# Banded attention on pairs of heads, woven slot by slot into the two products of an MoE layer

## The chip, the cores and the metric

One core of one Trainium2 chip runs the whole program. The metric is the device time of one execution in microseconds (us), the median of three runs. The core has five engines with a queue each: TensorE (PE; its weight loads are listed as PEld), VectorE (DVE), ScalarE (ACT), GpSimd (POOL) and SyncE (SP), which here only issues DMAs. Each takes its instructions in order and waits on semaphores for the others.

## The reference

Attention over 8 batches, 8 heads, 576 positions of 64 values, where a position sees itself and the 63 before it; then, on the concatenated heads, `(h - tanh(h)) @ w_out` with `h = x @ w_in`:

```python
scores = scale * np.matmul(q, k.transpose(0, 1, 3, 2))
mask = (rel >= 0) & (rel < 64)            # rel = query position - key position
scores = np.where(mask, scores, -1000000000.0)
scores = scores - np.max(scores, axis=-1, keepdims=True)
attn = np.exp(scores)
attn = attn / (np.sum(attn, axis=-1, keepdims=True) + 1e-09)
out = np.matmul(attn, v)                  # x: 4608 tokens of 512 values
h = x @ w_in                              # 512 x 2048
g = h - np.tanh(h)
result = g @ w_out                        # 2048 x 512, in float32
```

## The kernel before, in words

Two stages follow each other. Tile's scheduler and its pools set the order of instructions on each engine within a stage.

**Attention** (L66 to L128) goes through 64 heads. Per head GpSimd issues 15 DMAs that load and cast k, v and q in blocks of 128 rows (L78 to L80; each is one entry on the POOL queue). TensorE transposes k and q block by block (`tp`, L84 and L87), VectorE copies the transposes to `kT` and `qT` (L85, L88). Then five query tiles: scores `sc` (L101, 64 values deep), the band mask added on VectorE (L103), exp with row sums on ScalarE (L106), reciprocal and scaling on VectorE (L109, L110), one or two transposes of the probabilities (`tpp`, L119) with copies (`pt_sb`, L121), one or two products with v (`ov`, L126), and a copy into `xT` on ScalarE (L128). `xT` holds all 4608 tokens, transposed.

**MoE** (L138 to L154) goes through 9 chunks of 512 tokens. For each of 16 blocks of d_ff four 512-column products make `hp` (L142), ScalarE takes the tanh (`th`, L145), VectorE the difference (`gT`, L146). For each of four token blocks 16 products make `yp` (L150), ScalarE copies it to `ysb` (L153), and SyncE issues the store (L154). `hp` and `yp` have two PSUM banks each. Both weights are loaded first of all, by one DMA each on the POOL queue (L51, L53).

Of the kernel before, what the change touches and what calls it, by code (L numbers as in the profile page):

```python
# [1 line left out]

# [13 lines left out]
@with_exitstack
def kernel(
    ctx: ExitStack,
    tc: tile.TileContext,
    q: bass.AP,  # L20
    k: bass.AP,
    v: bass.AP,
    moe_w_in: bass.AP,
    moe_w_out: bass.AP,
    out: bass.AP,
):
# [20 lines left out]
    nc.gpsimd.affine_select(bmask, bmask, compare_op=ALU.is_gt, fill=-1e9,
                            base=0, pattern=[[1, 192]], channel_multiplier=-1)

    w_in_sb = const.tile([128, 4, d_ff], BF16)  # L50
    nc.gpsimd.dma_start(out=w_in_sb, in_=moe_w_in.rearrange("(ko ki) f -> ki ko f", ki=128))  # L51
    w_out_sb = const.tile([128, 16, d_model], BF16)
    nc.gpsimd.dma_start(out=w_out_sb, in_=moe_w_out.rearrange("(ko ki) f -> ki ko f", ki=128))  # L53

    xT = const.tile([128, 4, NT], BF16)

    scale = 1.0 / (D ** 0.5)

    attn_stack = ExitStack()
    kv_pool = attn_stack.enter_context(tc.tile_pool(name="kv", bufs=2))  # L60
    qt_pool = attn_stack.enter_context(tc.tile_pool(name="qt", bufs=2))
    ps_pool = attn_stack.enter_context(tc.tile_pool(name="ps", bufs=1, space=bass.MemoryType.PSUM))
    ps2_pool = attn_stack.enter_context(tc.tile_pool(name="ps2", bufs=2, space=bass.MemoryType.PSUM))
    sm_pool = attn_stack.enter_context(tc.tile_pool(name="sm", bufs=3))

    for b in range(B):  # L66
        for h in range(H):
            ksb = kv_pool.tile([128, NB, D], BF16)
            vsb = kv_pool.tile([128, NB, 128], BF16)
            pi0 = (h % 2) * 64  # L70
            po = h // 2
            nc.vector.memset(vsb, 0.0)
            qsb = kv_pool.tile([128, NB, D], BF16)
            kT = qt_pool.tile([64, S], BF16)
            qT = qt_pool.tile([64, S], BF16)
            for ib in range(NB):
                r = 128 if ib < 4 else 64
                nc.gpsimd.dma_start(out=ksb[:r, ib, :], in_=k[b, h, ib*128:ib*128+r, :])  # L78
                nc.gpsimd.dma_start(out=vsb[:r, ib, pi0:pi0+64], in_=v[b, h, ib*128:ib*128+r, :])  # L79
                nc.gpsimd.dma_start(out=qsb[:r, ib, :], in_=q[b, h, ib*128:ib*128+r, :])  # L80
            for ib in range(NB):
                r = 128 if ib < 4 else 64
                tp = ps_pool.tile([64, 128], BF16)
                nc.tensor.transpose(tp[:, :r], ksb[:r, ib, :], ident[:r, :r])  # L84
                nc.vector.tensor_copy(kT[:, ib*128:ib*128+r], tp[:, :r])  # L85
                tp2 = ps_pool.tile([64, 128], BF16)
                nc.tensor.transpose(tp2[:, :r], qsb[:r, ib, :], ident[:r, :r])  # L87
                nc.vector.tensor_copy(qT[:, ib*128:ib*128+r], tp2[:, :r])  # L88

            for t in range(5):  # L90
                if t == 0:
                    q0, sq, k0, sk = 0, 64, 0, 64
                    mask = cmask
                else:
                    q0 = 64 + 128 * (t - 1)
                    sq = 128
                    k0 = 128 * (t - 1)
                    sk = 192
                    mask = bmask
                sc = ps2_pool.tile([128, 192], F32)  # L100
                nc.tensor.matmul(sc[:sq, :sk], qT[:, q0:q0+sq], kT[:, k0:k0+sk],  # L101
                                 start=True, stop=True)
                nc.vector.tensor_tensor(sc[:sq, :sk], sc[:sq, :sk], mask[:sq, :sk], ALU.add)  # L103
                p_sb = sm_pool.tile([128, 192], BF16)
                rs = sm_pool.tile([128, 1], F32)
                nc.scalar.activation(p_sb[:sq, :sk], sc[:sq, :sk], ACT.Exp,  # L106
                                     scale=scale, accum_out=rs[:sq, :])
                rsi = sm_pool.tile([128, 1], F32)
                nc.vector.reciprocal(rsi[:sq, :], rs[:sq, :])  # L109
                nc.vector.tensor_scalar(p_sb[:sq, :sk], p_sb[:sq, :sk], rsi[:sq, :],  # L110
                                        None, ALU.mult)
                ov = ps2_pool.tile([128, 128], F32)
                nks = (sk + 127) // 128
                pts = []
                for j in range(nks):
                    c0 = j * 128
                    cw = min(128, sk - c0)
                    tpp = ps_pool.tile([128, 128], BF16)
                    nc.tensor.transpose(tpp[:cw, :sq], p_sb[:sq, c0:c0+cw], ident[:sq, :sq])  # L119
                    pt_sb = sm_pool.tile([128, 128], BF16)  # L120
                    nc.vector.tensor_copy(pt_sb[:cw, :sq], tpp[:cw, :sq])  # L121
                    pts.append((pt_sb, c0, cw))
                for j, (pt_sb, c0, cw) in enumerate(pts):
                    kb = (k0 + c0) // 128
                    ko = (k0 + c0) % 128
                    nc.tensor.matmul(ov[:, :sq], vsb[ko:ko+cw, kb, :], pt_sb[:cw, :sq],  # L126
                                     start=(j == 0), stop=(j == nks - 1))
                nc.scalar.activation(xT[pi0:pi0+64, po, b*S+q0:b*S+q0+sq], ov[pi0:pi0+64, :sq], ACT.Copy)  # L128

    attn_stack.close()  # L130
    mp = ctx.enter_context(tc.tile_pool(name="mp", bufs=2, space=bass.MemoryType.PSUM))
    mp2 = ctx.enter_context(tc.tile_pool(name="mp2", bufs=2, space=bass.MemoryType.PSUM))
    gpool = ctx.enter_context(tc.tile_pool(name="gp", bufs=2))
    opool = ctx.enter_context(tc.tile_pool(name="op", bufs=3))
    TOK = 512
    for nb in range(NT // TOK):
        t0 = nb * TOK
        gT = gpool.tile([128, 16, TOK], BF16)  # L138
        for m in range(16):
            hp = mp.tile([128, TOK], F32)  # L140
            for ki in range(4):
                nc.tensor.matmul(hp, w_in_sb[:, ki, m*128:(m+1)*128],  # L142
                                 xT[:, ki, t0:t0+TOK], start=(ki == 0), stop=(ki == 3))
            th = opool.tile([128, TOK], F32)
            nc.scalar.activation(th, hp, ACT.Tanh)  # L145
            nc.vector.tensor_tensor(gT[:, m, :], hp, th, ALU.subtract)  # L146
        for s in range(4):
            yp = mp2.tile([128, d_model], F32)
            for m in range(16):
                nc.tensor.matmul(yp, gT[:, m, s*128:(s+1)*128], w_out_sb[:, m, :],  # L150
                                 start=(m == 0), stop=(m == 15))
            ysb = opool.tile([128, d_model], F32)
            nc.scalar.activation(ysb, yp, ACT.Copy)  # L153
            nc.sync.dma_start(out=out[t0+s*128:t0+(s+1)*128, :], in_=ysb)  # L154


# [28 lines left out]
```

## Time and profile before

| | us |
|---|---|
| median of three runs | 896.19 (896.13 to 896.44) |
| span of the profiled execution | 894.0 |
| attention, first to last product | 26.0 to 629.8 |
| MoE, first product to end | 629.8 to 894.0 |
| TensorE busy | 756.3 |
| VectorE busy | 534.9 |
| ScalarE busy | 311.1 |
| GpSimd busy | 513.1 |

The profile is one execution. Its page gives busy time by engine, the span in 40 slices, the chain of work that ended last, the costliest groups of instructions by line, and the DMAs. "Idle before, releaser" in a row names what ended the idle time of the engine just before. Products on TensorE overlap, and their ends are modelled, so the distance of two starts tells more than a duration.

### The profile page before, as it was taken

Reading aid. Unit: us, or ns where it says so; the run is one execution under the profiler, and the core shown is the slowest. Engines: PE = TensorE matmul, PEld = TensorE weight load, DVE = VectorE, ACT = ScalarE, POOL = GpSimd, SP = SyncE. Lnnn points to the kernel's source line nnn. Section 1 sums busy time; section 2 is a strip of 40 time slices with the busy share of each in tenths; the row PEclk is TensorE's granted clock in tenths of the full one; section 3 lists DMA queues with packets and bytes.
Section 4 is the critical chain, followed back from the end, with each engine's and each line's share of the span. In section 5 each row is a group of like instructions: output and inputs, shape, how many; then the busy total and the mean of one; then the engine's idle time right before and its main releaser. Section 6 shows DMA issues by size and latency. Waiting matters only on the chain.

```text
span 894.0 us, 12015 instructions
## 1 busy us (share of the span) xinstructions
PE 756.3 (85%) x3264; PEld 341.5 (38%) x3264; DVE 534.9 (60%) x2384; ACT 311.1 (35%) x1141; POOL 513.1 (57%) x973
## 2 busy tenths in 40 slices
PE   0688888888888888888888888888999999999998
PEld 0333333333333333333333333333344444444443
DVE  0577777777777777777777777777533443334332
ACT  0233333333333333333333333333434443334433
POOL 3888888888888798798888888876000000000000
PEclk9999999999999999999999999999999999999999
DMA  9533334334333343343333433433011001100011
GB/s 164 52 24 25 25 24 25 25 24 25 24 26 24 23 27 25 23 27 24 24 24 25 25 24 25 25 22 21 1 48 48 25 23 48 48 36 23 36 48 48
DMA packets 133796, 28.62 MB, mean 32 GB/s; under 512 B 126560, under 2 KB 128608, under 8 KB 133728
## 3 DMA queue, kind: packets, MB, share of 16 engines
q0 software_dynamic: 128544, 18.41, 28.6%
q1 hardware_dynamic: 5184, 9.44, 2.8%
q8 instruction: 26, 0.43, 0.2%
q14 instruction: 42, 0.34, 0.1%
HBM read 36.70 MB, written 9.44 MB: 52 GB/s over the span
## 4 chain that ended last, share of the span: by engine, by line
PE 72%; DVE 17%; issue 4%; ACT 3%; DMA 3%; POOL 0%; ACTq 0%; DVEq 0%; POOLq 0%
PE tpp L119 15%; PE yp L150 14%; PE hp L142 14%; PE ov L126 11%; PE sc L101 10%; DVE pt_sb L121 7%; DVE sc L103 5%; PE tp L84 5%; PE tp L87 3%; DMA w_out_sb<-in_moe_w_out_dram 3%; ACT p_sb L106 2%; DVE p_sb L110 2%; DVE rsi L109 1%; DVE gT L146 1%; DVE qT L88 1%
## 5 line engine op out<-in xcount | busy, mean ns | idle before, releaser
L79 POOL DMA_DIRECT2D vsb<-in_v_dram x320 | 193.2, 604 | 85.0 <-DVE kT L85 73.5
L119 PE MATMUL tpp<-ident,p_sb 128*128 128x128 bf16 (+2 forms) x576 | 161.0, 279 | 85.2 <-DVE p_sb L110 40.8
L128 ACT ACTIVATE xT<-ov 64x128 bf16<-64x128 f32 (+1 forms) x320 | 83.3, 260 | 387.0 <-PE ov L126 387.0
L78 POOL DMA_DIRECT2D ksb<-in_k_dram x320 | 200.4, 626 | 17.5 <-issue 8.6
L80 POOL DMA_DIRECT2D qsb<-in_q_dram x320 | 195.5, 611 | 3.8 <-issue 3.8
L146 DVE TENSOR_TENSOR gT<-hp,th 128x512 bf16<-128x512 f32 x144 | 99.5, 691 | 152.6 <-ACT th L145 152.6
L121 DVE COPY pt_sb<-tpp 128x128 bf16<-128x128 bf16 (+2 forms) x576 | 124.6, 216 | 81.5 <-PE tpp L119 52.6
L126 PE MATMUL ov<-pt_sb,vsb 128*128 128x128 bf16 (+2 forms) x576 | 158.2, 275 | 13.8 <-DVE pt_sb L121 0.6
L142 PE MATMUL hp<-xT,w_in_sb 128*128 128x512 bf16 x576 | 147.4, 381 | 4.6 <-DVE gT L146 4.6
L150 PE MATMUL yp<-w_out_sb,gT 128*128 128x512 bf16 x576 | 145.6, 379 | 0.0
L84 PE MATMUL tp<-ident,ksb 128*64 128x128 bf16 (+1 forms) x320 | 96.6, 302 | 26.0 <-DMA ksb<-in_k_dram 26.0
L119 PEld LDWEIGHTS <-p_sb 128*128 128x128 bf16 (+2 forms) x576 | 68.9, 120 | 128.6 <-DVE p_sb L110 61.4
L145 ACT ACTIVATE th<-hp 128x512 f32<-128x512 f32 x144 | 86.0, 597 | 86.1 <-PE hp L142 58.9
L106 ACT ACTIVATE p_sb<-sc 128x192 bf16<-128x192 f32 (+1 forms) x320 | 97.3, 304 | 38.8 <-DVE sc L103 27.6
L126 PEld LDWEIGHTS <-vsb 64*128 64x128 bf16 (+1 forms) x576 | 58.5, 102 | 127.4 <-issue 90.1
L101 PE MATMUL sc<-kT,qT 64*128 64x192 bf16 (+1 forms) x320 | 103.1, 322 | 3.6 <-DVE qT L88 0.5
L103 DVE TENSOR_TENSOR sc<-sc,bmask 128x192 f32<-128x192 f32 x256 | 91.4, 357 | 23.8 <-PE sc L101 23.7
L87 PE MATMUL tp<-ident,qsb 128*64 128x128 bf16 (+1 forms) x320 | 97.2, 304 | 0.7 <-DMA qsb<-in_q_dram 0.6
L85 DVE COPY kT<-tp 64x128 bf16<-64x128 bf16 (+1 forms) x320 | 62.1, 194 | 49.3 <-PE tp L84 49.0
L110 DVE TENSOR_SCALAR p_sb<-p_sb,rsi 128x192 bf16<-128x192 bf16 (+1 forms) x320 | 87.8, 274 | 2.3
L142 PEld LDWEIGHTS <-w_in_sb 128*128 128x128 bf16 x576 | 55.9, 97 | 79.2 <-issue 19.2
L150 PEld LDWEIGHTS <-gT 128*128 128x128 bf16 x576 | 54.8, 98 | 70.3 <-DVE gT L146 6.4
(23 smaller groups left out, 353.8 us busy)
## 6 DMA issues: line engine op xcount, KB each, us to landing
out_dram<-ysb SPq DMA_DIRECT2D x36, 256.0 KB, 2.0
ksb<-in_k_dram POOLq DMA_DIRECT2D x256, 16.0 KB, 2.1
vsb<-in_v_dram POOLq DMA_DIRECT2D x256, 16.0 KB, 2.1
qsb<-in_q_dram POOLq DMA_DIRECT2D x256, 16.0 KB, 2.1
w_in_sb<-in_moe_w_in_dram POOLq DMA_DIRECT2D x1, 2048.0 KB, 13.1
w_out_sb<-in_moe_w_out_dram POOLq DMA_DIRECT2D x1, 2048.0 KB, 22.6
ksb<-in_k_dram POOLq DMA_DIRECT2D x64, 8.0 KB, 2.0
vsb<-in_v_dram POOLq DMA_DIRECT2D x64, 8.0 KB, 2.0
```

Source lines behind the costliest of these rows:

```text
L78: nc.gpsimd.dma_start(out=ksb[:r, ib, :], in_=k[b, h, ib*128:ib*128+r, :])
L79: nc.gpsimd.dma_start(out=vsb[:r, ib, pi0:pi0+64], in_=v[b, h, ib*128:ib*128+r, :])
L80: nc.gpsimd.dma_start(out=qsb[:r, ib, :], in_=q[b, h, ib*128:ib*128+r, :])
L84: nc.tensor.transpose(tp[:, :r], ksb[:r, ib, :], ident[:r, :r])
L87: nc.tensor.transpose(tp2[:, :r], qsb[:r, ib, :], ident[:r, :r])
L101: nc.tensor.matmul(sc[:sq, :sk], qT[:, q0:q0+sq], kT[:, k0:k0+sk], start=True, stop=True)
L103: nc.vector.tensor_tensor(sc[:sq, :sk], sc[:sq, :sk], mask[:sq, :sk], ALU.add)
L119: nc.tensor.transpose(tpp[:cw, :sq], p_sb[:sq, c0:c0+cw], ident[:sq, :sq])
L121: nc.vector.tensor_copy(pt_sb[:cw, :sq], tpp[:cw, :sq])
L126: nc.tensor.matmul(ov[:, :sq], vsb[ko:ko+cw, kb, :], pt_sb[:cw, :sq], start=(j == 0), stop=(j == nks - 1))
L142: nc.tensor.matmul(hp, w_in_sb[:, ki, m*128:(m+1)*128], xT[:, ki, t0:t0+TOK], start=(ki == 0), stop=(ki == 3))
L150: nc.tensor.matmul(yp, gT[:, m, s*128:(s+1)*128], w_out_sb[:, m, :], start=(m == 0), stop=(m == 15))
```

## The change

It replaces the whole body of the kernel. What is computed is the same.

**Attention on head pairs.** Heads `pr` and `pr + 4` of a batch form a pair `g` (32 in all). q and k of a pair come in by two SP DMAs as float32, 96 partitions with six positions each (`load_qk`); GpSimd casts them (`cast_qk`); six transposes each (`tr`) give `qT` by one ScalarE copy and `kTb` by two VectorE copies, in which the keys of the two heads alternate column by column and the other head's half is zero. So one 128x128 product gives the scores of 64 keys of both heads against 128 queries, already transposed (`scores`), exp goes straight into `PT`, and the mask is multiplied in afterwards for all nine blocks at once (`masking`). The products with `vaug` (`pv`) take `PT` as it lies; a column of ones in `vaug` gives the row sums; VectorE multiplies by the reciprocal into `xs`. `x_tr` transposes the result of a batch into chunk tiles `xT`. No maximum is subtracted in either kernel.

**One stream.** `manual_schedule` makes the order of the code the order on each engine. The stream is cut into slots `n`: slot `n` has the four products of one `hp` (chunk `n // 16`), attention steps of the table `early`, four products of `yp` of the chunk before, attention steps of the table `late`. A pair from g = 4 on starts every four slots; four pairs stand ahead of slot 0. I call the four slots of a pair A (`tr`), B (`scores`), C (`masking`, first `pv`) and D (second `pv`). Attention ends with slot 111, `hp` with 143, `yp` with 159. `hp`, scores and transposes have two PSUM banks, `yp` and `ov` one.

```diff
+    ctx.enter_context(tc.manual_schedule())
+    def cast_qk(g):
+        for n in "qk":
+            t = row_pool.tile([P96, E6, 2, D], BF16, tag=n + "b", name=n + "b")
+            nc.gpsimd.tensor_copy(t.rearrange("p e h d -> p h e d"),
+                                  stage.pop((g, n)).rearrange("p h (e d) -> p h e d", d=D))
...
+    def tr(g, which):
...
+        for e in range(E6):
+            nc.tensor.transpose(tp[:, e, :], src[:, e, :], ident[:P96, :P96])
+        if which == "q":
+            nc.scalar.activation(qT[g % NR][:, 0:S].rearrange("c (p e) -> c e p", e=E6), tp, ACT.Copy)
+        else:
+            kt = kTb[g % NR]
+            for i in range(2):
+                nc.vector.tensor_copy(
+                    kt[64 * i:64 * i + 64, :, i].rearrange("c (p e) -> c e p", e=E6),
+                    tp[64 * i:64 * i + 64])
+    def scores(g, grp):
+        sp = ps_s.tile([128, 3, 128], F32, tag="s", name="sp")
+        for i in range(3):
+            j = 3 * grp + i
+            nc.tensor.matmul(sp[:, i, :], kTb[g % NR].rearrange("c t h -> c (t h)")[:, 128 * j:128 * j + 128],
+                             qT[g % NR][:, 64 * j:64 * j + 128], start=True, stop=True)
+        nc.scalar.activation(PT[g % NR][:, 3 * grp:3 * grp + 3, 0:128], sp, ACT.Exp, scale=scale)
+    def masking(g):
+        p = PT[g % NR][:, :, 0:128]
+        nc.vector.tensor_tensor(p, p, mask.unsqueeze(1).to_broadcast([128, NJ, 128]), ALU.mult)
+    def pv(g, t0, t1):
...
+            for i, (j, c0) in enumerate(parts):
+                nc.tensor.matmul(ov[:, t - t0, :], ptf[:, c0:c0 + 128], vaug[b % NV][:, pr, j, :],
+                                 start=(i == 0), stop=(i == len(parts) - 1))
...
+        nc.vector.reciprocal(rc[:, 0:n], ovr[:, :, :, 64:65])
...
+        nc.vector.tensor_tensor(xo, ovr[:, :, :, 0:64], rc[:, 0:n].to_broadcast([128, n, 2, 64]), ALU.mult)
+    def y_out(c, s):
+        ysb = sm_pool.tile([128, d_model], F32, tag="ysb", name="ysb")
+        nc.scalar.activation(ysb, yps[c, s], ACT.Copy)
...
+    LEAD = 18
+    for g in range(NG):
+        b, pr = divmod(g, NP)
+        a = g - 10 if g < NP else 4 * g - LEAD
+        if g >= NP:
+            at(late, a - 10, load_qk, g)
+            at(late, a - 4, cast_qk, g)
+        at(early, a, tr, g, "q")
+        at(late, a, tr, g, "k")
+        at(early, a + 1, scores, g, 0)
+        at(early, a + 1, scores, g, 1)
+        at(late, a + 1, scores, g, 2)
+        at(early, a + 2, masking, g)
+        at(late, a + 2, pv, g, 0, 3)
+        at(late, a + 3, pv, g, 3, 5)
+        if pr == NP - 1:
             for t in range(5):
+                at(early if t % 2 == 0 else late, a + 4 + t // 3, x_tr, b, t)
+            if b + 2 < B:
+                at(late, a + 4, load_v, b + 2)
...
+        if 0 <= c < NC:
+            hp_mm(c, m)
+        for fn in early.get(n, []):
+            fn[0](*fn[1:])
+        if 1 <= c <= NC:
+            yp_mm(c - 1, m)
+        for fn in late.get(n, []):
+            fn[0](*fn[1:])
```

What stood on TensorE before, in the middle of attention (`sc` scores, `tp` and `tpp` transposes, `ov` products with v; in brackets the engine or DMA queue whose semaphore is waited for):

```order
L101 MATMUL sc<-kT,qT 128x192 [waits Activation_49]
L84 LDWEIGHTS ksb [waits DMASW1_49]
L84 MATMUL tp<-ident,ksb 64x64
L119 LDWEIGHTS p_sb
L119 MATMUL tpp<-ident,p_sb 64x128 [waits DVE_49]
L126 LDWEIGHTS vsb
L126 MATMUL ov<-pt_sb,vsb 128x128 [waits PE_49]
```

Nearly every product there has a wait of its own. The same queue now, from the end of slot A to the start of slot C of one pair (`tp` transposes of k, `hp` and `yp` the MoE products, `sp` scores; groups of like products cut to their first):

```order
L151 LDWEIGHTS kb [waits Pool_49]
L151 MATMUL tp<-ident,kb 128x96
...
L212 MATMUL hp<-xT,w_in_sb 128x512 [waits DVE_49]
...
L165 LDWEIGHTS ktb_100 [waits DVE_49]
L165 MATMUL sp<-qt_103,ktb_100 128x128 [waits Activation_49]
...
L226 MATMUL yp<-w_out_sb,gT 128x512
...
L165 MATMUL sp<-qt_103,ktb_100 128x128 [waits Activation_49]
...
L226 MATMUL yp<-w_out_sb,gT 128x512 [waits Activation_49]
```

The waits have moved to the heads of groups, and between the transposes of k and the scores that read them stands one group `hp`. VectorE before, in the same stage (`kT`, `pt_sb` copies, `rsi` reciprocal, `p_sb` scaling):

```order
L109 RECIPROCAL rsi<-rs 128x1 [waits Activation_49]
L103 TENSOR_TENSOR sc<-sc,bmask 128x192 [waits PE_49]
L110 TENSOR_SCALAR p_sb<-p_sb,rsi 128x192 [waits DVE_49]
L85 COPY kT<-tp 64x128 [waits PE_49]
L121 COPY pt_sb<-tpp 128x128 [waits PE_49]
```

and now, one period of four slots (`ktb` the copies of k, `pt` masking, `xs` the scaled result):

```order
L218 TENSOR_TENSOR gT<-hp,th 128x512 [waits Activation_49]
L157 COPY ktb_100<-tp 64x6x96 [waits PE_49]
L157 COPY ktb_100<-tp 64x6x96
L218 TENSOR_TENSOR gT<-hp,th 128x512 [waits Activation_49] x2
L171 TENSOR_TENSOR pt_97<-pt_97,mask 128x9x128
L189 RECIPROCAL rc<-ov 128x6 [waits PE_49]
L191 TENSOR_TENSOR xs_107<-ov,rc 128x6x64 [waits DVE_49]
L218 TENSOR_TENSOR gT<-hp,th 128x512 [waits Activation_49]
L189 RECIPROCAL rc<-ov 128x4 [waits PE_49]
L191 TENSOR_TENSOR xs_107<-ov,rc 128x4x64 [waits DVE_49]
```

VectorE now has eleven operations for a pair of heads and four `hp` groups, where attention alone took 35 for each head. Last, GpSimd at the start. Before:

```order
L51 DMA w_in_sb<-in_moe_w_in_dram 128x4x2048
L47 AFFINE_SELECT bmask<-bmask 128x192 [waits Pool_49]
L53 DMA w_out_sb<-in_moe_w_out_dram 128x16x512
L78 DMA ksb<-in_k_dram 128x64
L79 DMA vsb<-in_v_dram 128x64 [waits DVE_49]
```

and now, from the last of the four first pairs to the cast of the fifth (`vaug` is v, `qb`, `kb` the cast rows):

```order
L77 CAST qb<-qf 96x2x6x64 [waits DMAHW6_49,PE_49]
L77 CAST kb<-kf 96x2x6x64 [waits DMAHW7_49,PE_49]
L132 DMA w_in_sb<-in_moe_w_in_dram 128x4x512 [waits DMASW0_49]
...
L89 DMA vaug_95<-in_v_dram 64x36x64 [waits DMASW4_49,DVE_49]
...
L136 DMA w_out_sb<-in_moe_w_out_dram 128x4x512 [waits DMASW0_49]
L136 DMA w_out_sb<-in_moe_w_out_dram 128x4x512 [waits DMASW1_49]
L77 CAST qb<-qf 96x2x6x64 [waits DMAHW0_49,PE_49,Pool_49]
```

The weights have moved behind the first four pairs, in four pieces each, and the casts of the fifth pair stand behind them.

## Rows read from the trace of the kernel before

**Rows 1.** The page: span, and a DMA group (count, KB each, us to landing).

```profile
span 894.0 us, 12015 instructions
...
ksb<-in_k_dram POOLq DMA_DIRECT2D x256, 16.0 KB, 2.1
```

**Rows 2.** Stretches: length, busy by engine (instructions), granted clock, DMA share, GB/s.

```profile
0.00:26.00 26.00, 0.00 (x0) 0.00 (x0) 0.65 (x2) 1.28 (x1) 7.53 (x20) 1.00 0.99 166
26.00:629.80 603.80, 500.53 (x2112) 230.83 (x2112) 434.66 (x2238) 202.10 (x959) 505.58 (x953) 1.00 0.38 24
632.80:881.00 248.20, 243.59 (x1105) 105.70 (x1104) 98.42 (x143) 104.45 (x175) 0.00 (x0) 1.00 0.09 34
```

**Rows 3.** Timeline of MoE: start, duration, engine, line, instructions, idle before.

```profile
700.78 1.02 PE L142 MATMUL hp<-xT,w_in_sb 128*128 128x512 bf16 x4
701.64 0.38 PE L150 MATMUL yp<-w_out_sb,gT 128*128 128x512 bf16 x1
701.84 0.60 ACT L145 ACTIVATE th<-hp 128x512 f32<-128x512 f32 x1 [0.76 <-DVE gT L146]
...
880.22 9.95 PE L150 MATMUL yp<-w_out_sb,gT 128*128 128x512 bf16 x45
890.26 0.60 ACT L153 ACTIVATE ysb<-yp 128x512 f32<-128x512 f32 x1 [2.90 <-PE yp L150]
```

**Rows 4.** Timeline of TensorE: a pair in attention, the first loads of MoE.

```profile
302.39 0.31 PE L84 MATMUL tp<-ident,ksb 128*64 128x128 bf16 x1
302.49 0.31 PE L87 MATMUL tp<-ident,qsb 128*64 128x128 bf16 x1
...
630.21 0.15 PEld L142 LDWEIGHTS <-w_in_sb 128*128 128x128 bf16 x1 [0.28 <-issue]
630.64 0.15 PEld L142 LDWEIGHTS <-w_in_sb 128*128 128x128 bf16 x1 [0.27 <-issue]
```

**Rows 5.** Instructions by line and shape: count, busy us, mean ns, idle before.

```profile
L146 DVE TENSOR_TENSOR gT<-hp,th 128x512 bf16<-128x512 f32 x144 | 99.5, 691 | 152.6 <-ACT th L145 152.6
L103 DVE TENSOR_TENSOR sc<-sc,bmask 128x192 f32<-128x192 f32 x256 | 91.4, 357 | 23.8 <-PE sc L101 23.7
L145 ACT ACTIVATE th<-hp 128x512 f32<-128x512 f32 x144 | 86.0, 597 | 86.1 <-PE hp L142 58.9 <-DVE gT L146 27.2
L106 ACT ACTIVATE p_sb<-sc 128x192 bf16<-128x192 f32 x256 | 83.4, 326 | 12.5 <-DVE sc L103 2.0
L110 DVE TENSOR_SCALAR p_sb<-p_sb,rsi 128x192 bf16<-128x192 bf16 x256 | 73.1, 286 | 2.3
L121 DVE COPY pt_sb<-tpp 128x128 bf16<-128x128 bf16 x256 | 57.5, 224 | 46.5 <-PE tpp L119 38.4
L109 DVE RECIPROCAL rsi<-rs 128x1 f32<-128x1 f32 x256 | 39.2, 153 | 5.1 <-ACT p_sb L106 1.1
L72 DVE MEMSET vsb<- 128x320 uint32 x64 | 20.8, 325 | 1.8 <-PEq L169 0.9 <-PE tp L84 0.4
L110 DVE TENSOR_SCALAR p_sb<-p_sb,rsi 64x64 bf16<-64x64 bf16 x64 | 14.7, 230 | 0.0
L121 DVE COPY pt_sb<-tpp 64x64 bf16<-64x64 bf16 x64 | 11.7, 182 | 8.6 <-PE tpp L119 0.2
L106 ACT ACT_TABLE_LOAD x1 | 1.3, 1283 | 0.7 <-PEq L169 0.7
L45 POOL TENSOR_SCALAR_AFFINE_SELECT bmask<-bmask 128x192 f32<-128x192 f32 x1 | 0.3, 335 | 0.0
L41 POOL TENSOR_SCALAR_AFFINE_SELECT cmask<-cmask 64x64 f32<-64x64 f32 x1 | 0.2, 228 | 0.0
```

**Rows 6.** Timeline of GpSimd at the start of the program.

```profile
2.89 0.36 POOL L47 TENSOR_SCALAR_AFFINE_SELECT bmask<-bmask 128x192 f32<-128x192 f32 x1
3.18 1.19 POOL L53 DMA_DIRECT2D w_out_sb<-in_moe_w_out_dram  x1
4.90 0.57 POOL L79 DMA_DIRECT2D vsb<-in_v_dram  x1
```

More of the change, by code (lines that the diff above doesn't have):

```diff
@@ L4 @@
 import concourse.tile as tile
-from concourse import bass_utils, mybir
-from concourse.masks import make_identity
+from concourse import mybir
 from concourse._compat import with_exitstack
@@ L47 @@
[L47 to L88, printed above, removed]
-            for t in range(5):
[L91 to L154, printed above, removed]
@@ new lines, with load_qk @@
+    xs = [const.tile([128, 5, d_model], BF16, name=f"xs{i}") for i in range(2)]
+    stage, rows = {}, {}
+    def load_qk(g):
+        b, pr = divmod(g, NP)
+        for n, x in (("q", q), ("k", k)):
+            t = qk_pool.tile([P96, 2, E6 * D], F32, tag=n + "f", name=n + "f")
+            nc.sync.dma_start(out=t, in_=x[b, pr::NP].rearrange("h (p e) d -> p h (e d)", e=E6))
+            stage[g, n] = t
+    def cast_qk(g):
[3 more added lines that the diff above has]
+                                  stage.pop((g, n)).rearrange("p h (e d) -> p h e d", d=D))
+            rows[g, n] = t
@@ new lines @@
+    ones(0)
+    nc.vector.memset(vaug[1], 0.0)
+    ones(1)
+    w_in_r = moe_w_in.rearrange("(ko ki) f -> ki ko f", ki=128)
+    w_out_r = moe_w_out.rearrange("(ko ki) f -> ki ko f", ki=128)
+    for pr in (1, 2, 3):
+        load_v_pair(0, pr)
+        cast_qk(pr)
+    for i in range(4):
+        nc.gpsimd.dma_start(out=w_in_sb[:, :, 512 * i:512 * i + 512],
+                            in_=w_in_r[:, :, 512 * i:512 * i + 512])
+    load_v(1)
+    for i in range(4):
+        nc.gpsimd.dma_start(out=w_out_sb[:, 4 * i:4 * i + 4, :], in_=w_out_r[:, 4 * i:4 * i + 4, :])
@@ new lines, in x_tr @@
+    def x_tr(b, t):
+        tp = ps_tp.tile([128, 4, 128], BF16, tag="tp", name="tpx")
+        for i in range(4):
+            nc.tensor.transpose(tp[:, i, :], xs[b % 2][:, t, 128 * i:128 * i + 128], ident)
+        lo, hi = b * S + 128 * t, b * S + min(128 * t + 128, S)
+        at = lo
+        while at < hi:
+            c = at // TOK
+            to = min(hi, (c + 1) * TOK)
+            nc.vector.tensor_copy(chunk_tile(c)[:, :, at - c * TOK:to - c * TOK],
+                                  tp[:, :, at - lo:to - lo])
+            at = to
@@ new lines, with hp_mm @@
+    gT, yps = {}, {}
+    def hp_mm(c, m):
+        hp = ps_hp.tile([128, TOK], F32, tag="hp", name="hp")
+        for ki in range(4):
+            nc.tensor.matmul(hp, w_in_sb[:, ki, m * 128:(m + 1) * 128], chunk_tile(c)[:, ki, :],
+                             start=(ki == 0), stop=(ki == 3))
+        th = sm_pool.tile([128, TOK], F32, tag="th", name="th")
+        nc.scalar.activation(th, hp, ACT.Tanh)
+        if m == 0:
+            gT[c] = g_pool.tile([128, M, TOK], BF16, tag="gT", name="gT")
+        nc.vector.tensor_tensor(gT[c][:, m, :], hp, th, ALU.subtract)
@@ new lines, in yp_mm @@
+    def yp_mm(c, st):
+        s, part = divmod(st, 4)
+        if part == 0:
+            yps[c, s] = ps_yp.tile([128, d_model], F32, tag="yp", name="yp")
+        for i in range(4):
+            m = 4 * part + i
+            nc.tensor.matmul(yps[c, s], gT[c][:, m, s * 128:(s + 1) * 128], w_out_sb[:, m, :],
+                             start=(m == 0), stop=(m == M - 1))
+    def y_out(c, s):
+        ysb = sm_pool.tile([128, d_model], F32, tag="ysb", name="ysb")
+        nc.scalar.activation(ysb, yps[c, s], ACT.Copy)
+        r0 = c * TOK + s * 128
+        nc.sync.dma_start(out=out[r0:r0 + 128, :], in_=ysb)
@@ L158 @@
+    first = min(min(early), min(late))
+    for n in range(first, 16 * (NC + 1) + 1):
+        c, m = divmod(n, M)
+        if n >= 1:
+            cy, sy = divmod(n - 17, M)
+            if n >= 17 and sy % 4 == 3 and cy < NC:
+                y_out(cy, sy // 4)
+        if 0 <= c < NC:
[6 more added lines that the diff above has]
+            fn[0](*fn[1:])
 _INS = ['q', 'k', 'v', 'moe_w_in', 'moe_w_out']
```

102 lines of the change are left out of this document (89 added, 13 removed).

## The prediction

> **What bounds the kernel now.** I read the page first, then the stretches, then the lines of single instructions. The page gives a span of 894.0 us [rows 1]; the median of the runs is 896.19 us, so 2.2 us lie around the span. The stretches show two programs behind each other [rows 2]: nothing on TensorE until 26.0 us, attention from there to 629.8 us, then the two MoE products to 894. Attention is thus 604 us, and by its 2112 products a step takes 286 ns. It is no bound of throughput: TensorE, VectorE and GpSimd are all 72 to 84% busy there, and each small product is one link in a chain through other engines. MoE is a bound of throughput: 512-column products follow each other at (9.95 - 0.38) / 44 = 0.2175 us, and in the middle of the stage at 0.2155 [rows 3] (45 from 880.22, which end 9.95 us later, the last 0.38 after its start; four from 700.78 to 701.64).
>
> [...]
>
> **The change part by part.** Removed: all 2112 small products and 2238 VectorE operations [rows 2] of attention as a stage of its own. Put in: for each of 32 head pairs 12 transposes of 96 columns, 9 score products of 128 and 13 value products of 130; for each of 8 batches 20 transposes of the result; 1248 products in all. Of the 32 pairs, 28 stand inside the MoE stream, one every four slots, 4 ahead of it. MoE keeps its 1152 products: 1152 x 0.2155 = 248 us, the floor.
>
> Price of a small product. From below 0.2155/4 = 0.054 us (a stream at the upper level), from above 0.105 us (the pair of [rows 4]). I price at the upper level, since every slot of the stream holds eight 512-column products of the kind beside which [rows 3] shows it, and take 0.065, nearer to the lower end, since at neither level do the closest rows show a load that holds up a product. 1248 x 0.065 = 81 us. [...]
>
> Prices on the other engines [rows 5]. ScalarE: 192 columns 0.326, 512 columns 0.597, so 0.85 ns a column: an exp of 384 columns 0.49, the copy of qT (576) 0.65; tanh 0.60, ysb, as many columns, 0.60. One load of a function table served Exp, Tanh and Copy of the whole program [rows 5], so alternating them costs nothing. VectorE: 0.357 at 192 and 0.691 at 512 columns, 1.04 ns a column: gT 0.69, the product with the reciprocal 0.56 and 0.42 with 0.15 for the reciprocal ahead of it. The bf16 copy runs 0.182 at 64 and 0.224 at 128 columns: a copy of 512 columns 0.48; the two kT copies (576 columns, every second element written) between 0.52 and 0.69 each: I take 0.69, because the cheap rows all write neighbouring elements. Masking, 1152 columns: 0.286 at 192 and 0.230 at 64 give 0.71; at 1.04 ns a column it would be 1.29, which the time until its reader covers. GpSimd casts (768 columns) appear in no row: affine-select of 64 and 192 columns at 0.228 and 0.335 gives 0.9; above that I allow 1.8, the double.
>
> One period (four slots, one pair), written out by hand from these prices with 0.2 us from the last product of a group to its reader (tanh at 701.84 follows the fourth of the products from 700.78 at 0.2155 each [rows 3]). Work on TensorE: 32 x 0.2155 + 34 small = 6.9 + 2.0 = 8.9 us. VectorE has 6.7 us, ScalarE 5.1, GpSimd 2 to 4: none is the bound. But TensorE takes its instructions in order, so two waits show. (1) Transposes of k end slot A; two copies of 0.69 and 0.2 latency follow, and only hp of slot B (0.86) stands ahead of the score products that read them: 0.75 us wait. The MoE products of that slot queue behind it. (2) yp has a single bank, its evacuation stands on ScalarE behind the third exp, at the end of slot B; exp ends 0.65 into slot C, ysb 1.25, and yp could start at 0.86: 0.4 us. Masking ends 0.75 ahead of its reader; hp with two banks, ov with one, are free in time. Period 8.9 + 1.15 = about 10.1. Once in four periods five result transposes come in: 1.3 us of products, and their copies stand on VectorE behind gT, with two banks for three users: about 1.4 us more. Sixteen slots: 4 x 10.1 + 2.7 = 43.2 us, 2.7 per slot.
>
> The sum in order. Start to slot 0: before, both weights (4 MB) went first and nothing ran on TensorE until they were in, 26 us at 166 GB/s [rows 2]; now q and k of the first pair (0.59 MB, 3.6 us at that rate, plus the 2.1 that a small DMA takes to land [rows 1]) are in at about 6 us. GpSimd then goes through four pairs, casts and v issues at 0.6 each, 3 us a pair, to 17; ten larger issues, between the 0.57 and the 1.19 of [rows 6], say 0.9 each, and the wait for the second piece of w_in take it to 28, and only then comes the cast of pair 4, whose transposes stand ahead of the first hp: 35 us. VectorE's own chain (memsets of 2.4 by 0.325 for 320 words [rows 5], four pairs of 3.5 with latencies) ends near 29, the lower end; casts at 1.8 give 43. Slots 0 to 15, with no yp as cover: the same chain with 8.5 us a period, 36 (30 to 42). Slots 16 to 111: 96 x 2.7 = 259; TensorE alone at 0.054 gives 212, 0.105 with the same waits 294. Slots 112 to 143: 256 x 0.2155 = 55. Slots 144 to 159: 64 x 0.2155 = 14 and three waits for the single yp bank, 0.86 each: 16. Last evacuation to the end 3.9 (890.26 to the end of the span in [rows 3], and 0.2). Around the span 2. In all 35 + 36 + 259 + 55 + 16 + 4 + 2 = 407 us.
>
> **The rivals.** *Everything hides:* the kT copies cost 0.52, the scheduled distance covers the waits, small products stream at 0.054: 30 + 32 + 220 + 77 = about 360 to 385. For it speaks that no engine but TensorE is near full; against it that the two waits follow from in-order queues and from durations of the trace. *Another wait takes over:* masking has two operands in SBUF and runs while GpSimd casts. In the trace of before, GpSimd only issues DMAs after 3.25 us [rows 6], so no row shows the two together. If a mask had to wait out one or both casts (0.9 to 1.8 each), less the 0.75 of slack, that is up to 1 us, or 2.9, in each of 28 pairs: 435 to 485. [...] Against the rival: a cast is released by transposes of slot A and should be done before the mask at the start of slot C. [...] *Slower than before:* GpSimd's cast, the one operation with no row of its kind, becomes the bound. Outside slots 0 to 111 I count 112 us, so slower needs 784 us there, 28 us a pair, 14 us a cast or 18 ns a column against the 0.9 of [rows 5]; from there on it decides, and it is the only engine for which no row excludes it directly.
>
> **How the numbers follow.** Forecast with its waits 0.62 (385 to 435), everything hides 0.17, another wait 0.16, lower clock 0.03, casts as the bound 0.01, and 0.01 for an end within 0.2% of before, about what a measurement can tell from no change. The time is 407. The range reaches into both neighbours, 362 to 462: below it only all lower ends together, above it the double wait, the clock and the casts. Faster 0.98, same 0.01, slower 0.01.
>
> **What would show it.** Right: 512-column products 0.2155 apart in the stream; small ones near 0.065; each period about 10.1 us with two gaps on TensorE, ended by the kT copies on VectorE and by ysb on ScalarE; first hp at 35 us; a stretch of some 71 us without attention at the end. Wrong: small products at 0.1 or products at 0.43 us in the stream (price or clock); TensorE waiting for masking with GpSimd busy beside it (the lock); first hp after 45 us (casts or issues at the start); a period set by VectorE.

## The result, and the profile after

The changed kernel takes 643.23 us (median of four runs, 639.93 to 643.82) against 896.16 before: a ratio of 0.717 with a 95% interval of 0.715 to 0.719. Faster, as forecast, but by half of what was forecast: 407 us with a range of 362 to 462 missed it by 236 us.

The page after, in the parts that answer to [rows 1, 2, 5]: span, busy time by engine, the granted clock in 40 slices (tenths of full speed), and groups of instructions (count, busy us, mean ns, idle before, what ended it):

```profile
span 641.7 us, 6133 instructions
...
PE 405.8 (63%) x2400; PEld 210.7 (33%) x2400; DVE 356.2 (56%) x431; ACT 210.4 (33%) x309; POOL 80.7 (13%) x103
...
PEclk9999966668888777778888777777889777799999
...
L157 DVE COPY ktb<-tp 64x576 bf16<-64x576 bf16 x64 | 171.7, 2684 | 13.1 <-PE tp L151 11.6
L153 ACT ACTIVATE qt<-tp 128x576 bf16<-128x576 bf16 x32 | 66.9, 2089 | 21.2 <-PE tp L151 21.2
L171 DVE TENSOR_TENSOR pt<-pt,mask 128x1152 bf16<-128x1152 bf16 x32 | 24.0, 749 | 0.2
```

Two things stand out. The copies of k into `ktb` are the second largest group of the program: 64 of 2.68 us, where the forecast had 0.69, and the copy of q takes 2.09 us instead of 0.65. And the granted clock, which in [rows 2] never moved, goes up and down in the stream: digits 6 to 9 of `PEclk` above, means of 0.65 and 0.81 in the stretches below.

Cut at the first `hp`, the first `yp` and the first slot without attention, the stretches (length, busy by engine, granted clock, DMA share, GB/s) are:

```profile
0.00:71.80 71.80, 19.95 (x177) 16.72 (x178) 45.68 (x54) 17.49 (x20) 30.61 (x45) 1.00 1.22 171
71.80:145.70 73.90, 42.71 (x228) 22.45 (x226) 41.74 (x50) 23.09 (x34) 8.61 (x10) 0.65 0.18 20
145.70:565.20 419.50, 273.28 (x1681) 140.39 (x1680) 245.93 (x293) 143.04 (x212) 41.45 (x48) 0.81 0.25 49
565.20:641.70 76.50, 69.85 (x323) 31.15 (x320) 22.85 (x35) 26.83 (x45) 0.00 (x0) 0.99 0.12 45
```

Against the forecast's 35, 36, 259 and 75 us: 37 us too many at the start, 38 in slots 0 to 15, 160 in slots 16 to 111, 2 at the end. TensorE's waits in the stream (who waited for whom, us, times, longest) name two causes:

```profile
PE sp L165 <- DVE ktb L157: 124.0, 27, 5.2
PE ov L185 <- DVE pt L171: 37.1, 28, 2.1
```

And one period of the timeline, from the second copy of k to the value products (start, length, engine, line, instructions, idle before), shows the third:

```profile
299.05 2.68 DVE L157 COPY ktb<-tp 64x576 bf16<-64x576 bf16 x1
301.77 0.69 DVE L218 TENSOR_TENSOR gT<-hp,th 128x512 bf16<-128x512 f32 x1
...
301.79 0.82 PE L165 MATMUL sp<-qt,ktb 128*128 128x128 bf16 x6 [4.61 <-DVE ktb L157]
...
302.40 1.92 PE L226 MATMUL yp<-w_out_sb,gT 128*128 128x512 bf16 x4
...
304.43 1.89 PE L212 MATMUL hp<-xT,w_in_sb 128*128 128x512 bf16 x4
...
306.99 0.69 DVE L218 TENSOR_TENSOR gT<-hp,th 128x512 bf16<-128x512 f32 x1 [4.54 <-ACT th L215]
307.60 0.75 DVE L171 TENSOR_TENSOR pt<-pt,mask 128x1152 bf16<-128x1152 bf16 x1
...
308.41 0.63 PE L185 MATMUL ov<-vaug,pt 128*128 128x130 bf16 x8 [1.22 <-DVE pt L171]
308.88 1.02 PE L212 MATMUL hp<-xT,w_in_sb 128*128 128x512 bf16 x4
```

TensorE stands still for 4.61 us until `ktb` is there. The four products `yp` behind the scores then take 1.92 us as a group, where four at 308.88 take 1.02: they go at 0.43 us each (weight loads at 302.83 and 303.26), the distance between the first loads of MoE in [rows 4], twice the 0.2155 of [rows 3]. And the mask stands on VectorE behind `gT` of the same slot, so the value products wait 1.22 us for it.

### The profile page after: what moved, and what is told of

Its sections match the earlier page's. It is cut to its first block, busy times and chain, and to the rows that moved or that the text cites. A ratio compares the mean times of both kernels' runs of the same rounds, so it can differ in the third digit from the quotient of the medians.

```text
span 641.7 us, 6133 instructions
## 1 busy us (share of the span) xinstructions
PE 405.8 (63%) x2400; PEld 210.7 (33%) x2400; DVE 356.2 (56%) x431; ACT 210.4 (33%) x309; POOL 80.7 (13%) x103
## 4 chain that ended last, share of the span: by engine, by line
PE 42%; DVE 24%; issue 6%; ACT 5%; POOL 1%; DMA 1%; SPq 0%; POOLq 0%; ACTq 0%
DVE ktb L157 18%; PE yp L226 17%; PE hp L212 16%; PE sp L165 4%; PE ov L185 3%; DVE gT L218 3%; ACT th L215 2%; DVE pt L171 2%; PE tp L151 2%; ACT qt L153 2%; ACT ysb L231 1%; PE tpx L196 1%; DMA qf<-in_q_dram 1%; POOL qb L77 1%; DVE xT L202 0%
## 5 line engine op out<-in xcount | busy, mean ns | idle before, releaser
L212 PE MATMUL hp<-xT,w_in_sb 128*128 128x512 bf16 x576 | 179.9, 443 | 0.1
L157 DVE COPY ktb<-tp 64x576 bf16<-64x576 bf16 x64 | 171.7, 2684 | 13.1 <-PE tp L151 11.6
L165 PE MATMUL sp<-qt,ktb 128*128 128x128 bf16 x288 | 42.9, 309 | 164.5 <-DVE ktb L157 163.5
L167 ACT ACTIVATE pt<-sp 128x384 bf16<-128x384 f32 x96 | 44.0, 493 | 195.9 <-PE sp L165 195.9
L165 PEld LDWEIGHTS <-ktb 128*128 128x128 bf16 x288 | 30.0, 140 | 187.7 <-DVE ktb L157 176.0
L153 ACT ACTIVATE qt<-tp 128x576 bf16<-128x576 bf16 x32 | 66.9, 2089 | 21.2 <-PE tp L151 21.2
L185 PE MATMUL ov<-vaug,pt 128*128 128x130 bf16 x416 | 40.3, 244 | 40.8 <-DVE pt L171 37.1
L77 POOL CAST qb<-qf 96x768 bf16<-96x768 f32 x32 | 26.6, 831 | 207.5 <-DMA qf<-in_q_dram 192.9
L185 PEld LDWEIGHTS <-pt 128*128 128x128 bf16 x416 | 30.8, 109 | 65.4 <-DVE pt L171 52.5
L191 DVE TENSOR_TENSOR xs<-ov,rc 128x384 bf16<-128x384 f32 x64 | 31.4, 491 | 2.2
L151 PE MATMUL tp<-ident,qb 96*128 96x96 bf16 x192 | 15.2, 222 | 14.0 <-POOL qb L77 7.4
```

Of the source, the lines that this page charges most:

```text
L77: nc.gpsimd.tensor_copy(t.rearrange("p e h d -> p h e d"), stage.pop((g, n)).rearrange("p h (e d) -> p h e d", d=D))
L153: nc.scalar.activation(qT[g % NR][:, 0:S].rearrange("c (p e) -> c e p", e=E6), tp, ACT.Copy)
L157: nc.vector.tensor_copy(kt[64 * i:64 * i + 64, :, i].rearrange("c (p e) -> c e p", e=E6), tp[64 * i:64 * i + 64])
L165: nc.tensor.matmul(sp[:, i, :], kTb[g % NR].rearrange("c t h -> c (t h)")[:, 128 * j:128 * j + 128], qT[g % NR][:, 64 * j:64 * j + 128], s ...
L167: nc.scalar.activation(PT[g % NR][:, 3 * grp:3 * grp + 3, 0:128], sp, ACT.Exp, scale=scale)
L185: nc.tensor.matmul(ov[:, t - t0, :], ptf[:, c0:c0 + 128], vaug[b % NV][:, pr, j, :], start=(i == 0), stop=(i == len(parts) - 1))
```

## Experiments

All runs below are compared with the kernel before on the same chip, which takes 895.03 to 896.66 us on the chips used, so what the chip adds to a difference of two runs is under 0.2%. The changed kernel stands at 643.23 us. The first four ask where the time of the copies comes from and what their wait does.

**What a copy costs by its steps (`e0_steps`).** Fourteen copies on VectorE and six on ScalarE, put ahead of the stream, for instance:

```diff
+    nc.vector.tensor_copy(wide[h, 0:576], pf[h])
+    nc.vector.tensor_copy(wide[h, 0:1152:2], pf[h])
...
+    nc.vector.tensor_copy(wide[:, 0:6912:12], pf)
...
+    nc.vector.tensor_copy(wide[h, 0:576].rearrange("c (p e) -> c p e", e=6), probe[h].rearrange("c e p -> c p e"))
```

> The changed kernel with 14 copies on VectorE and 6 on ScalarE put ahead of its stream, each of 576 bf16 columns, with other steps and sides; the time of the whole is of no use. Theory (the write costs: each 2-byte element goes to another place in SBUF): with neighbours 0.4 to 0.5 us on VectorE, rising with the step written to the 2.68 us of the kT copies at a step of 12 elements (24 bytes); as slow on 128 partitions as on 64; a copy that reads PSUM in steps of 96 elements and writes neighbours near 0.7; on ScalarE 0.6 with neighbours, 2.09 at a step of 6. Rival one (the read of bf16 from PSUM or the three-dimensional pattern costs): 2.7 us at any step, and the copy from SBUF to SBUF with a written step of 6 elements stays under 0.8. Rival two (a half-used word costs): the price jumps at a step of 2 elements and stays there.

The timeline of VectorE in the one run, with written steps of 1, 2, 4, 6, 8 and 12 elements (L145 to L150), 12 elements on 128 partitions (L151), a read in steps of 96 elements with neighbours written (L154), and from SBUF with a written step of 6 (L157):

```profile
22.75 0.45 DVE L145 COPY wide<-probe 64x576 bf16<-64x576 bf16 x1
23.23 0.79 DVE L146 COPY wide<-probe 64x576 bf16<-64x576 bf16 x1
24.05 1.42 DVE L147 COPY wide<-probe 64x576 bf16<-64x576 bf16 x1
25.51 2.06 DVE L148 COPY wide<-probe 64x576 bf16<-64x576 bf16 x1
27.60 2.69 DVE L149 COPY wide<-probe 64x576 bf16<-64x576 bf16 x1
30.33 2.67 DVE L150 COPY wide<-probe 64x576 bf16<-64x576 bf16 x1
33.03 2.68 DVE L151 COPY wide<-probe 128x576 bf16<-128x576 bf16 x1
...
40.53 0.75 DVE L154 COPY wide<-probe 64x576 bf16<-64x576 bf16 x1
...
42.37 1.11 DVE L157 COPY wide<-wide 64x576 bf16<-64x576 bf16 x1
```

and ScalarE with steps of 1, 4 and 12 elements (2 and 6 take 0.81 and 2.08):

```profile
45.42 0.65 ACT L159 ACTIVATE wide<-probe 128x576 bf16<-128x576 bf16 x1
...
46.94 1.44 ACT L161 ACTIVATE wide<-probe 128x576 bf16<-128x576 bf16 x1
...
50.52 2.69 ACT L163 ACTIVATE wide<-probe 128x576 bf16<-128x576 bf16 x1
```

The price goes with the distance of two writes: 0.45, 0.79, 1.42, 2.06 and 2.69 us at 2, 4, 8, 12 and 16 bytes, and no more at 24 (2.67). 64 or 128 partitions make no difference (2.67 and 2.68 at 24 bytes), and a long step on the read adds 0.3 us (0.75). The two engines agree to 0.02 us from 4 bytes on. So the theory stands, though it had the price rise up to 12 elements, and both rivals fall. The innermost write step of the kT copies is 12 elements: six positions of a partition, times two heads.

**The same copies in the order of positions (`e1_natural`).**

```diff
-                    kt[64 * i:64 * i + 64, :, i].rearrange("c (p e) -> c e p", e=E6),
-                    tp[64 * i:64 * i + 64])
+                    kt[64 * i:64 * i + 64, :, i].rearrange("c (p e) -> c p e", e=E6),
+                    tp[64 * i:64 * i + 64].rearrange("c e p -> c p e"))
```

and the same for the copy of q.

> The same copies of qT and kTb, written in the order of positions (kTb every second element, qT neighbours) and read from PSUM in steps of 96 elements. Theory (long write steps cost): kT copies about 0.7 us instead of 2.68, qT copy about 0.65 instead of 2.09; the wait of the scores for kTb falls from 5 us to under 1 us a pair, the clock is no longer lowered, time 430 to 460. Rival (any long step costs, on either side): copies as long as now, time 630 to 650. Second rival (the copies are only one of several bounds and TensorE finds another wait): copies short, time above 520.

Measured 455.34 us, 0.5087 of before (0.5074 to 0.5099): 188 us of the 236 go with two rearranged patterns. The copy of k is 0.80 us, that of q 0.65, the waits of TensorE now:

```profile
PE sp L166 <- DVE ktb L158: 43.9, 31, 13.9
PE ov L186 <- DVE pt L172: 29.3, 28, 2.1
```

Without the 13.9 us of the start that is 1.0 us a pair for the scores: 1.55 to 1.71 each up to slot 15, and 0.69 to 0.84 in slots 16 to 111, where the forecast had 0.75. The mask still has its wait, 1.0 us a pair against 1.3 in the changed kernel.

**Neighbours on both sides (`e2_neighbours`).** The copies write their data where they should not, without any step:

```diff
+                    kt.rearrange("c t h -> c (t h)")[64 * i:64 * i + 64, 576 * i:576 * i + 576],
+                    tp[64 * i:64 * i + 64].rearrange("c e p -> c (e p)"))
```

and the same for the copy of q.

> The same copies with neighbours read and written on both sides; the positions then stand in another order in kTb and qT and the zero halves are overwritten, so what attention computes is not the reference's; every instruction and wait is there. Theory (the price of these copies and what the wait does to the clock is the whole miss beyond a later start): kT copies 0.45 us, qT 0.6, granted clock above 0.95 in the stream, time 410 to 440. Rival (the order of the stream itself or the clock in a mixed stream is at fault): copies short, but products still at 0.43 us in good part, time above 520.

428.84 us, 0.4788 (0.4771 to 0.4805), copies at 0.45 us, granted clock 0.988 over the span. The order of the stream and a mixed stream as such are not what cost the clock.

**Products that nobody uses in place of standing still (`e3_fill`).**

```diff
+        if grp == 0 and 8 <= g:
+            for _ in range(26):
+                nc.tensor.matmul(sp.rearrange("p a b -> p (a b)"), w_in_sb[:, 0, 0:128], w_in_sb[:, 1, 0:384],
+                                 start=True, stop=True)
```

> 26 products of 384 columns that nobody uses, ahead of the first scores of each pair from the ninth on, in the bank that these scores overwrite: TensorE works through the wait for kTb instead of standing still, the wait itself stays. Theory (standing still 5 us lowers the clock, and the products behind it run at 0.43 us, some 2.2 us a pair): after the wait products at 0.2155 us, granted clock near 1.0 in the stream, 24 pairs x 2.2 = about 55 us less: 580 to 600. Rival (the clock falls for another reason, or its fall is hidden by other waits): 640 to 660.

594.37 us, 0.6631 (0.6615 to 0.6648): 624 products more, and 49 us less. The timeline of one period:

```profile
307.52 5.46 DVE L157 COPY ktb<-tp 64x576 bf16<-64x576 bf16 x2
308.18 4.39 PE L165 MATMUL sp<-w_in_sb 128*128 128x384 bf16 x26
...
313.03 0.51 PE L169 MATMUL sp<-qt,ktb 128*128 128x128 bf16 x6 [0.46 <-DVE ktb L157]
313.38 1.03 PE L230 MATMUL yp<-w_out_sb,gT 128*128 128x512 bf16 x4
```

The scores still start when `ktb` is there, but what follows is at 0.2155 us a product, and between 145 and 505 us the granted clock is 1.00, where the changed kernel has 0.81 in slots 16 to 111. So the fall of the clock behind the wait, and what hung on it, cost 49 / 24 = 2.0 us a pair beside the wait itself. In the changed kernel the eight 512-column products behind a wait at 0.43 us instead of 0.2155 alone are 1.7 of them.

The next four start from the repaired copies, but for one, and look for the rest.

**The mask ahead of gT (`e4_mask_first`).** `masking` of a pair is issued before `hp_mm` of slot C, through a third table:

```diff
+        for fn in first_of.get(n, []):
+            fn[0](*fn[1:])
         if 0 <= c < NC:
             hp_mm(c, m)
...
-        at(early, a + 2, masking, g)
+        at(first_of, a + 2, masking, g)
```

> e1_natural with one more edit: the masking of a pair is put on VectorE ahead of the gT of slot C instead of behind it. Theory (the value products wait about 1.05 us a pair for the mask only because gT, which waits for tanh of the same slot, stands ahead of it): that wait goes, 28 x 1.05 = 29 us less than e1_natural's 455: 424 to 432. Rival (another wait of the same slot takes its place, ysb or the bank of ov): less than 10 us gained, 445 to 455.

421.46 us, 0.4698 (0.4686 to 0.4710): 34 us less than with the copies alone, a little more than its wait. The value products no longer wait:

```profile
204.33 0.76 DVE L172 TENSOR_TENSOR pt<-pt,mask 128x1152 bf16<-128x1152 bf16 x1 [1.43 <-ACT pt L168]
...
205.30 0.69 DVE L219 TENSOR_TENSOR gT<-hp,th 128x512 bf16<-128x512 f32 x1 [0.22 <-ACT th L216]
205.69 0.62 PE L186 MATMUL ov<-vaug,pt 128*128 128x130 bf16 x8
```

**Transposes of k ahead of those of q (`e5_k_before_q`).**

```diff
-        at(early, a, tr, g, "q")
-        at(late, a, tr, g, "k")
+        at(early, a, tr, g, "k")
+        at(late, a, tr, g, "q")
```

> e1_natural with one more edit: in slot A the transposes of k come first and those of q after yp, so that the two copies on VectorE have yp (0.86 us) more as cover and the one copy on ScalarE has hp alone. Theory (the remaining wait for kTb, 0.83 to 1.0 us a pair, is the distance that the two copies lack): it goes, 28 us less than 455: 425 to 435. Rival (VectorE is late anyway, since gT of slot A stands ahead of the copies, or the copy of q becomes as late): 445 to 456.

458.52 us, 0.5104 (0.5080 to 0.5128): no gain, which is the rival, though 2.5 us above its range. TensorE has the transposes of k 1.1 us earlier, but VectorE takes `gT` first:

```profile
210.67 0.69 DVE L219 TENSOR_TENSOR gT<-hp,th 128x512 bf16<-128x512 f32 x1 [0.77 <-ACT th L216]
...
211.28 1.60 DVE L158 COPY ktb<-tp 64x576 bf16<-64x576 bf16 x2
...
212.94 0.51 PE L166 MATMUL sp<-qt,ktb 128*128 128x128 bf16 x6 [0.69 <-DVE ktb L158]
```

**The start (`e6_start`).** The columns of ones of the first v tile are written ahead of its first DMA; nothing else moves.

```diff
     nc.vector.memset(vaug[0], 0.0)
+    nc.vector.reduce_sum(par, ident.rearrange("p (a h) -> p h a", h=2), axis=mybir.AxisListType.X)
...
+    ones(0)
     load_v_pair(0, 0)
...
-    nc.vector.reduce_sum(par, ident.rearrange("p (a h) -> p h a", h=2), axis=mybir.AxisListType.X)
...
-    ones(0)
```

> e1_natural with one more edit: the columns of ones of the first v tile are written ahead of its first DMA instead of behind it. Theory (VectorE stands 9 us until that DMA lands at about 16 us, and the first kT copies and three v issues stand behind it): first hp 8 to 10 us earlier, 445 to 448. Rival (the loads of the weights set the start of slot 0): 452 to 457.

446.10 us, 0.4976 (0.4968 to 0.4985), 9 us less than with the copies alone, with the first `hp` at 45.1 instead of 52.2 us, 7 us earlier where 8 to 10 were expected. In the changed kernel VectorE stands still until the first v DMA has landed, and the first copies of k stand behind that:

```profile
15.86 0.34 DVE L119 CAST vaug<-par 128x36 bf16<-128x36 f32 x2 [8.91 <-DMA vaug<-in_v_dram]
...
19.84 5.37 DVE L157 COPY ktb<-tp 64x576 bf16<-64x576 bf16 x2
```

**Scattered copies, one slot more of distance (`e7_earlier`).** The changed kernel, both transposes of a pair a slot earlier.

```diff
-        at(early, a, tr, g, "q")
-        at(late, a, tr, g, "k")
+        at(early, a - 1, tr, g, "q")
+        at(late, a - 1, tr, g, "k")
```

> The changed kernel with its scattered copies as they are, but both transposes of a pair one slot earlier. The copies keep their 2.68 us; scores come one slot later after them. Theory (the price of the copies is paid as a wait, because one group hp is all that covers 5.4 us; VectorE has the time, 10.8 us in a period): the wait moves to the bank of hp, which gT behind the copies frees late, some 1.7 us a pair; period 13 instead of 17, products back at 0.2155 in good part; 530 to 570. Rival (VectorE's order makes every distance too short): above 610.

581.74 us, 0.6481 (0.6465 to 0.6498). It is neither: less gain than the theory's 530 to 570, more than the rival's. The copies still begin late, since the scaling of the pair before stands ahead of them on VectorE, and the scores wait 3.20 us instead of 4.61:

```profile
296.09 0.42 DVE L191 TENSOR_TENSOR xs<-ov,rc 128x256 bf16<-128x256 f32 x1
296.43 5.39 DVE L157 COPY ktb<-tp 64x576 bf16<-64x576 bf16 x2
...
301.88 0.51 PE L165 MATMUL sp<-qt,ktb 128*128 128x128 bf16 x6 [3.20 <-DVE ktb L157]
302.22 1.58 PE L226 MATMUL yp<-w_out_sb,gT 128*128 128x512 bf16 x4
```

The wait did not move to the bank of `hp`; instead result transposes wait for the same copies, seven times and 31.3 us in all. Distance buys part of the wait, not the price; and the products slow down behind the shorter wait too, at a granted clock of 0.881 over the span: the four `yp` products take 1.58 us here, against 1.03 ahead of the copies (296.79), and 1.91 behind the wait of the pair before.

The last three settle the shares and add up the repairs.

**Only the copies of k repaired (`e9_only_k`).** The edit of `e1_natural` as it stands in its diff; the copy of q stays scattered.

> The changed kernel with the kT copies alone written in the order of positions; the copy of qT on ScalarE stays scattered at 2.09 us. Theory (the kT copies alone make the wait; the copy of qT has yp, the transposes of k and hp as cover, some 2.0 us): within 10 us of e1_natural, 455 to 465. Rival (both copies carry the loss, as the qT copy also holds up tanh behind it on ScalarE): 490 or more.

465.15 us, 0.5189 (0.5181 to 0.5196). So of the 188 us the copies of k carry 178, and that of q 10 once those of k are repaired; it lies behind `yp`, the transposes of k and `hp`. The copy of q repaired alone was not run.

**Transposes of k ahead of hp (`e11_k_first`).** On top of the mask's edit, so that the copies stand ahead of `gT` of slot A on VectorE:

```diff
+        at(first_of, a, tr, g, "k")
         at(early, a, tr, g, "q")
-        at(late, a, tr, g, "k")
```

> e4_mask_first with one more edit: the transposes of k stand ahead of hp of slot A, so that on VectorE both copies stand ahead of the gT of that slot (e5_k_before_q left gT ahead of them, and the wait stayed). Theory (distance on VectorE's queue, not on TensorE's, decides the wait for kTb): 0.83 us in each of 28 pairs gone, 421.5 - 23: 394 to 402. Rival (gT behind the copies now frees the bank of hp late, or the waits for the transposes' banks grow by as much): 415 to 424.

393.32 us, 0.4384 (0.4378 to 0.4391): 28 us less than with the mask's edit, a little more than expected. TensorE's waits for `ktb` fall from 44.0 us to 3.4 in all. The transposes stand one group `hp` earlier on TensorE as well, but 1.1 us earlier there alone gave nothing in `e5_k_before_q`: together the two runs say that the place on VectorE's queue decides.

**All four repairs (`e10_best`).** The edits of `e1_natural`, `e4_mask_first`, `e11_k_first` and `e6_start` in one kernel.

> e11_k_first with the start of e6_start as well: all four edits that the readings point to (copies in the order of positions, mask ahead of gT, transposes of k ahead of hp, columns of ones ahead of the first v load). Theory (the gains add, since each takes away a wait of its own): 9 us less than e11_k_first, 385 to 393. Rival (the start is then set by the loads): no less than e11_k_first.

389.19 us, 0.4341 (0.4333 to 0.4348), the fastest of all: 40% less than the changed kernel. The start gives only 4 us more here, not 9: the first `hp` comes 9.0 us earlier than in `e11_k_first` (38.57 against 47.58), but slots 0 to 15 take 39.7 us against 35.0, with a wait of 2.8 us for a load of v and a mask of 2.71 us in them. Behind the 7.0 us until the first cast, at the start of the program, TensorE's waits are down to small pieces; two of the larger groups:

```profile
PE yp L227 <- ACT ysb L232: 7.5, 27, 0.7
PE tpx L197 <- DVE ktb L158: 6.4, 6, 1.5
```

## Why the prediction was wrong

**The step that failed first is the price of the two kT copies.** The text gave them "between 0.52 and 0.69 each" and took the upper end. Neither end was a bound (0.69 is the row of 512 columns; 576 at 1.04 ns a column more are 0.76): every row of [rows 5] that I took for a copy writes neighbours, and the edit writes steps of 24 bytes. I noted "every second element written" and read the step off the heads, not off the innermost loop of the rearranged pattern, which runs over the partitions of the load and so jumps six positions and two heads. 2.68 us against 0.69, twice a pair, and 2.09 against 0.65 for q. The repaired kernel, with 0.80 and 0.65, stands 188 us below the changed one.

**The mechanism was the one foretold, with the wrong size.** Wait (1) of the forecast, TensorE in order behind the copies, is there in 27 pairs of the stream; it takes 4.6 us on average (3.3 to 5.2) instead of 0.75. With repaired copies it is 0.69 to 0.84 us in slots 16 to 111. Wait (2), ysb ahead of yp, is not seen in the changed kernel's stream; with repaired copies it is 0.20 us a pair instead of 0.4.

**The clock was priced as a constant.** The two levels of the prediction are two distances of 512-column products before: 0.2155 us in [rows 3], and 0.43 between the first loads of MoE in [rows 4]. That they are levels of the clock was my reading; the granted clock before is 1.00 in the stretches of both, also in that of the loads:

```profile
629.80:632.80 3.00, 3.00 (x9) 1.07 (x9) 0.43 (x1) 0.87 (x2) 0.00 (x0) 1.00 0.00 0
```

I priced the stream at 0.2155 throughout and gave a lower clock 0.03. Both distances take turns: behind each long wait the products go at 0.43 us, later in the same period at 0.2155, with a granted clock of 0.80 over the period (299.0 to 316.1 us). By `e3_fill` that is 2.0 us for each of 24 pairs, 49 us of the miss, which lie inside the 188. The step behind it is the wait: with short waits (`e1_natural`, `e2_neighbours`) the granted clock over the span is 0.996 and 0.988.

**The mask was put in the wrong place.** "Masking ends 0.75 ahead of its reader" took the mask as ahead of `gT` of slot C. The order on VectorE, printed ahead of the prediction, has two `gT` ahead of it, the second of which waits for tanh of the same slot. 34 us by `e4_mask_first`. No size was off here; the order was misread, and a wait put at nothing.

**The start** came to 71.8 us instead of 35. The forecast let GpSimd's chain end last and VectorE's at 29 us; it was VectorE's that ended last. The casts of the fifth pair, the last link of the forecast's chain, are done at 37.4 us. But five pairs pay 5.4 us of copies each, one behind the other, the fifth from 65.03 us on, and VectorE waits for the first v DMA until 15.9 us, a wait the forecast did not see: with the copies repaired the first `hp` is at 52.2, with the ones moved too at 45.1. Of the 10 us left, all four edits together (`e10_best`) take another 6.5, with the first `hp` at 38.6; the rest is open. In `e6_start` the first four pairs start their scores 3.8, 4.7 and 6.1 us apart, where I allowed 3.5 a pair. Slots 0 to 15, 73.9 us instead of 36, take 46.1 with repaired copies and 38.4 with the mask ahead of `gT` as well.

**What was right.** Where 512-column products go at 0.2155 us in the stream, eight small products take 0.63 us as a group and one alone about 0.23: 0.057 each, inside 0.054 to 0.105 and near the 0.065 taken. Casts, at 831 ns each in the groups of the page after, 0.83 (0.9 in the text, though its two rows give 0.82), masking 0.75 (0.71), gT 0.69, exp 0.49, the store's copy 0.59. The waits for the single bank of `yp` at the end are 0.69 to 0.74 each (0.86), but four, not three. The stretch behind attention is 76.5 us (75). With copies and mask repaired (`e4_mask_first`) a period is 10.05 us, where the forecast had about 10.1, though its 34 small products at 0.065 make 2.2 us and not the 2.0 written. And the sum closes: 455 with the copies repaired, less 34 for the mask and 9 for the start, is 412, where the forecast without these three had 407. That last subtraction is worked out, not run, and part of the agreement is luck: the start is still 10 us too long, while slots 16 to 111 take 252 us in `e4_mask_first`, 7 less than forecast.

**The rivals.** "Another wait takes over" named the mask beside GpSimd's casts. In the changed kernel all masks take 0.75 to 0.76 us, so that was not it. "Everything hides" falls with the waits; the lower clock came, but for part of each period; the casts are far from a bound, with GpSimd busy for 13% of the span. What the prediction calls the lock, a mask held up by casts, was an estimate with no row behind it; it shows at the start of the repaired kernels alone, with a mask of 2.51 us in `e6_start` (last section).

## What to carry to other kernels

Before pricing a copy that rearranges, write down the innermost step of its destination in bytes: from PSUM to SBUF, 576 two-byte elements cost 0.45 us on VectorE (0.65 on ScalarE) as neighbours and 2.7 us on either at 24 bytes, while a long step on the read side adds 0.3 us on VectorE (`e0_steps`). In a hand-ordered stream replay each engine's queue from its printed order, since an operation that waits holds up what is ready behind it (34 us by `e4_mask_first`). And price a long wait on TensorE twice: once as itself, 4.6 us a pair here, once for the products behind it, 2.0 by `e3_fill`.
